# A recurrence with a capacity-dropped mixture of experts: one operand written out by ScalarE, a group's last unit fetched alone, inversion steps in four slots, late weights behind the second gather

## The chip, the cores and the metric

The kernel runs on one core of a Trainium2 chip. The metric is the device time of one execution in microseconds; lower is better. The median of three runs of the kernel before is 619.46 us (617.57 to 620.58).

## The reference, cut to what matters

The first part is a recurrence over 768 tokens for 4 batches and 8 heads with a state of 40 x 40. The second part takes its output as 3072 rows of 320, sends each row to one of 8 experts, keeps the 80 rows with the largest gate per expert, and leaves the other rows zero.

```python
for t in range(S):                                  # S = 768
    y[:, :, t] = einsum('bhd,bhde->bhe', r_t, state)
    Sa = einsum('bhde,bhe->bhd', state, a_t)
    state = state * w_t[:, :, None, :] - einsum('bhd,bhe->bhde', Sa, b_t)
    state = state + einsum('bhd,bhe->bhde', v_t, k_t)
x = y.transpose(0, 2, 1, 3).reshape(3072, 320)
logits = x @ w_gate;  expert_idx = argmax(logits, axis=1)
gate_w = softmax(logits)[arange(N), expert_idx]
for e in range(8):
    tok_idx = rows of expert e, the 80 of largest gate_w
    out[tok_idx] = gate_w[tok_idx] * (maximum(x[tok_idx] @ w1[e], 0) @ w2[e])
```

## The kernel before, in words

**Units and groups.** The recurrence is cut into chunks of 64 tokens. A unit is one chunk of two batches with all eight heads; there are 24 units, n = 0 to 23. Within a chunk the recurrence becomes a triangular system, whose matrix is called N (tile `nt`). Its diagonal blocks of 32 x 32 are inverted by elimination on VectorE, for four units at once (NG = 4): such a set of units is a group, with index k = n // 4. The elimination of a group has 30 steps, each two VectorE instructions (`step`, L381 and L384) on the tiles `lt` (the blocks) and `tt` (the inverse being built).

**The way of the blocks.** `system_kept` copies a unit's N from PSUM into `nt` on ScalarE (L352) and writes it to a DRAM tensor `blocks` with two DMAs on SP's queue (L355). When the last unit of a group has been written, `fetch` reads the blocks of all four units back as `lt`, one unit's heads on eight partitions of each block row, with four DMAs on SP (L365). `begin` makes `tt` from `lt` on GpSimd (L370). After the last step `end` writes `tt` to DRAM (`solved`, L387) and reads it back turned as `dt` (L392), both on SP. TensorE multiplies with `dt` in `diagonal` (L453).

**The order.** Each engine works through its instructions in the order in which the function `do` lays them down; SP's DMAs and those that ScalarE issues belong to that order too. The loop runs over n. In iteration n, unit n is solved, unit n - 1 is read out and its state updated, and unit m = n + 7 (AHEAD) is prepared, with the decays of m + 1. SP's loads in one iteration are, in order: `raw_w`, `blocks`, (`lt`), `raw_a`, four `raw_s`, (`solved`, `dt`), two `x_rows`, `raw_r`, `side` and, in eight iterations, a zero fill of `out`. A load of a buffer waits for the instruction that read the buffer last.

VectorE's order in an iteration is two scans (`forward`, `backward`), `decayed_a` (`ahT`), a few steps, `inverted` (`scaled`), more steps, and `summed` with `state` (L522) and `xT` (L526). The PSUM tile `yp` that `xT` reads is free for the next unit's first matmuls (L416) only after it. How many steps run is decided by `pause(steps, budget)`: it takes steps from the list until their prices exceed the budget.

```python
            if not coming:
                pause(steps, 9 if n % NG == 1 else 5.5 if n % NG == 2 else 100)
                pause(rounds_, LISTS.get(n, 0))
            elif n % NG == 0:
                do(begin, m // NG)
            else:
                pause(steps, 6.7 if n % NG < NG - 1 else 100)
```

**The start.** Before the loop, units 0 to 7 are prepared by `prepare` and `joined`, and the first group is inverted while the other engines wait for it.

**After the loop.** The gates of all rows are merged into lists of the best 80 per expert, while the weights of experts 0 to 2 are read. A chain of small instructions turns the lists into row numbers (`idx_g`). Matmuls that nobody reads (`keep_at_work`, L146, on the tile `late`) keep TensorE busy. GpSimd then gathers the rows of each expert with an indirect DMA (`gather`, L932), and TensorE does the two matrix products of each expert (`first_half` L955 and L962, `second_half` L972). A DMA of `idx_g` into a DRAM tensor `held` stands in SP's queue ahead of the weights of experts 3 to 7, so these are requested only once the row numbers exist.

Of the kernel before, what the change touches and what calls it, by code (L numbers as in the profile page):

```python
# [18 lines left out]
def kernel(  # L19
# [46 lines left out]
    assert G * ZT == 512 and NG * 32 == 128 and E == 8 and 1 <= cap <= 128  # L66
# [66 lines left out]
    ones_b = const.tile([128, 128], BF16, name="ones_b")  # L133
    behind_b = const.tile([128, 128], BF16, name="behind_b")
    seg_t = const.tile([128, E, 2 * NM], F32, name="seg")
    seg = seg_t.rearrange("p e m -> p (e m)")
    iot = const.tile([128, 1, cap], F32, name="iot")


# [7 lines left out]

    nc.gpsimd.tensor_copy(ones_b, ones)
    nc.gpsimd.tensor_tensor(out=behind_b, in0=strict, in1=ones, op=Alu.subtract)
    nc.gpsimd.memset(seg_t, 1.0)  # L150
    nc.gpsimd.memset(seg_t[:, :, 0:1], 0.0)
    iot_i = const.tile([128, cap], I32, name="iot_i")
    nc.gpsimd.iota(iot_i, pattern=[[1, cap]], base=1, channel_multiplier=0)
    nc.gpsimd.tensor_copy(iot[:, 0, :], iot_i)


    with ExitStack() as p1:
# [190 lines left out]
        def system_kept(n):  # L348
            o = of[n]
            p = o.pop("np")  # L350
            o["nt"] = nt = kept.tile([128, Z, 2 * G, T], F32, name="nt", tag="nt", bufs=AHEAD + 1)
            nc.scalar.copy(nt.rearrange("p z (q g) t -> p q z (g t)", q=2), p.rearrange("p q z g t -> p q z (g t)"))  # L352

            for i, m in enumerate(halves):
                nc.sync.dma_start(blocks[n // NG, m, n % NG], nt[m, 1 - i])  # L355
            for z, m in enumerate(halves):
                masked(nt[m, z])


        def fetch(k):  # L360
            inverse[k]["lt"] = lt = sb.tile([128, C * C], F32, name="lt", tag="lt")
            for i in range(Z):
                for j in range(NS):
                    m = block(i, j)
                    nc.sync.dma_start(lt[m].rearrange("p (s t) -> p s t", s=C),  # L365
                                      blocks[k, m, :, :, j * C : (j + 1) * C].rearrange("s u h t -> (u h) s t"))
# [183 lines left out]
        def logits_summed(n):  # L550
            i = share_of[n]
            nc.vector.tensor_reduce(logit[i][:, n - shares[i][0], :], of[n]["xb"][:, :, 2 * D :].rearrange("p g e -> p e g"),  # L552
                                    axis=AX, op=Alu.add)
            of[n].clear()
# [137 lines left out]
        def joined(n):  # L692
            do(operand, n)
            do(system, n)
            do(system_kept, n)

        def prepare(n, before=None, next_=True):
# [10 lines left out]
            if before is not None:  # L708
                do(system, before)
                do(system_kept, before)  # L710
            if next_:
# [11 lines left out]
        do(fetch, 0)  # L723
# [18 lines left out]
        for n in range(NU + 2):  # L742
# [24 lines left out]
            if coming:  # L767
                do(system_kept, m)
                if m % NG == NG - 1:
                    do(fetch, m // NG)  # L770
# [4 lines left out]
            if next_:  # L775
                do(turned_a, m + 1)
                do(decayed_a, m + 1)
            pause(small, 1)
            pause(steps, 0.7)
# [16 lines left out]
            if not coming:  # L796
                pause(steps, 9 if n % NG == 1 else 5.5 if n % NG == 2 else 100)
                pause(rounds_, LISTS.get(n, 0))
            elif n % NG == 0:
                do(begin, m // NG)  # L800
            else:
                pause(steps, 6.7 if n % NG < NG - 1 else 100)
# [19 lines left out]
            if coming and m % NG == NG - 1:  # L822
                invert(m // NG)
# [10 lines left out]
    pieces = const.tile([128, NM, NP, E], BF16, name="pieces")  # L834
    rest = const.tile([128, NM, E], F32, name="rest")
    for x, last, first_piece in ((ids, 1, 0), (gates, 4, 2)):
        for i in range(first_piece, last):
            nc.gpsimd.tensor_copy(pieces[:, :, i, :], x)
            nc.gpsimd.tensor_tensor(out=rest if i + 1 < last else pieces[:, :, last, :], in0=x, in1=pieces[:, :, i, :], op=Alu.subtract)
            x = rest  # L840

# [21 lines left out]
    with ExitStack() as p2:  # L863
# [46 lines left out]
        keep_at_work(ps_l, "still", 40, late)  # L910
# [71 lines left out]
    held = nc.dram_tensor("held", (cap, E), I32, kind="Internal")  # L982
    nc.sync.dma_start(held[:, :], idx_g)
# [37 lines left out]
```

## Time and profile before

| What | Before |
|---|---|
| Median of three runs | 619.46 us (617.57 to 620.58) |
| Profiled execution: own time, span | 620.17 us, 618.5 us |
| Mean granted TensorE clock | 0.871 |
| Busy: TensorE, VectorE, ScalarE, GpSimd | 480.6, 362.5, 234.7, 130.2 us |
| DMA: packets, of these under 512 B | 236033, 217236 |
| Inversion steps: 360 VectorE instructions, all groups | 136.4 us |

The span runs from the first to the last instruction of the program. A line of the timeline gives the start, the duration, the engine, the line of the kernel, the operation, the tiles written and read, the count of merged instructions, and in brackets the idle time of the engine before it with what ended it. A "q" after an engine's name marks its instruction queue, as in SPq, where DMAs are issued. In the list of waits the numbers are microseconds in total, times, and the longest one.

### The profile page before, as it was taken

The page shows a single profiled execution, that of the slowest core. Times are in us where ns is not written, and L with a number is a line of the kernel's source. Part 1 is how long each engine was busy: PE and PEld are TensorE (multiplying, and loading weights), DVE is VectorE, ACT ScalarE, POOL GpSimd, SP SyncE. Part 2 cuts the span into 40 slices and gives each one's busy share as a digit, 9 for nine tenths or more (in the row PEclk, how much of TensorE's full clock was granted, in tenths as well). Part 3 has the DMA queues.
Part 4 walks back from the last instruction along what each step waited for, and adds up shares of the span by engine and source line. Part 5 has one row for each costly group of instructions (what it writes and reads, how often), then busy time and mean ns, then how long its engine had stood idle before and what let it go on. Part 6 is the DMA issues. An engine that isn't in the chain of part 4 may idle for free. (4 is left out here: it accounts for less than half of the span.)

```text
span 618.5 us, 25228 instructions
## 1 busy us (share of the span) xinstructions
PE 480.6 (78%) x11281; PEld 411.2 (66%) x11281; DVE 362.5 (59%) x870; ACT 234.7 (38%) x418; POOL 130.2 (21%) x171
## 2 busy tenths in 40 slices
PE   2874039978979898978998898599888205999996
PEld 1653037867869787877887787488777204877874
DVE  8766932678547874888567853988266984001010
ACT  2462015645654655655564554154445000000000
POOL 5022003222221412422231133021112012111011
PEclk9986557989996989999998899799999556579999
DMA  4587077535777658765766345125210179995000
GB/s 75 109 165 134 11 122 124 95 64 116 137 122 145 133 128 153 144 140 96 141 113 121 73 87 103 33 70 79 49 33 14 21 258 347 330 334 158 14 14 14
DMA packets 236033, 71.46 MB, mean 116 GB/s; under 512 B 217236, under 2 KB 228756, under 8 KB 235924
## 3 DMA queue, kind: packets, MB, share of 16 engines
q1 hardware_dynamic: 223728, 66.47, 49.6%
q10 hardware_dynamic: 11428, 1.73, 1.7%
q8 instruction: 89, 1.46, 0.9%
q0 software_dynamic: 768, 1.64, 0.9%
q14 instruction: 20, 0.16, 0.1%
HBM read 51.69 MB, written 18.12 MB: 113 GB/s over the span
## 5 line engine op out<-in xcount | busy, mean ns | idle before, releaser
L272 POOL TENSOR_SCALAR_AFFINE_SELECT side<-side 64x1024 f32<-64x1024 f32 x47 | 55.3, 1176 | 113.0 <-ACT side L500 111.7
L384 DVE TENSOR_TENSOR tt<-tt,tmp 128x30 f32<-128x30 f32 (+9 forms) x180 | 71.2, 396 | 6.6
L381 DVE TENSOR_TENSOR tmp<-tt,lt 128x30 f32<-128x30 f32 (+9 forms) x180 | 65.2, 362 | 14.5 <-POOL tt L370 9.3
L272 POOL TENSOR_SCALAR_AFFINE_SELECT nt<-nt 64x512 f32<-64x512 f32 x48 | 34.4, 717 | 139.6 <-ACT nt L352 138.3
L416 PE MATMUL yp<-rT,gT 64*64 64x64 f32 x768 | 30.6, 231 | 35.9 <-DVE lg L552 28.2
L416 PEld LDWEIGHTS yp<-rT,gT 64*64 64x64 f32 x768 | 27.7, 145 | 37.8 <-issue 35.6
L319 ACT COPY qd<-qt 128x1024 f32<-128x1024 f32 x24 | 25.3, 1053 | 71.6 <-DVE qt L305 68.1
L974 DVE TENSOR_SCALAR y<-yp,weight 80x320 f32<-80x320 f32 x8 | 4.4, 548 | 79.4 <-PE yp L972 79.4
L522 DVE TENSOR_TENSOR state<-yp,pt 64x320 f32<-64x320 f32 x44 | 21.4, 487 | 50.1 <-PE yp L518 49.8
L518 PE MATMUL yp<-side,scaled 128*64 128x128 f32 (+1 forms) x768 | 47.5, 279 | 2.2 <-POOL side L272 2.2
L245 PE MATMUL tp<-ident,raw_a 128*128 128x128 f32 x96 | 19.2, 333 | 35.4 <-DMA raw_a<-in_a_dram 35.0
L518 PEld LDWEIGHTS yp<-side,scaled 128*64 128x64 f32 x768 | 41.9, 143 | 3.9 <-POOL side L272 2.4
L298 DVE TENSOR_TENSOR_SCAN pt<-decay,begins 128x520 f32<-128x520 f32 x24 | 30.3, 1263 | 20.2 <-ACT decay L292 20.0
L453 PE MATMUL pr<-yy,dt 32*32 32x40 f32 x1536 | 39.0, 203 | 3.7 <-ACT yy L446 1.8
L453 PEld LDWEIGHTS pr<-yy,dt 32*32 32x32 f32 x1536 | 32.6, 111 | 10.9 <-issue 5.7
L972 PE MATMUL yp<-w,hT 128*80 128x320 f32 x128 | 38.5, 448 | 0.0
L245 PEld LDWEIGHTS tp<-ident,raw_a 128*128 128x128 f32 x96 | 12.4, 166 | 38.5 <-issue 34.7
L966 ACT ACTIVATE hT<-hp 128x320 f32<-128x320 f32 x16 | 6.1, 434 | 83.3 <-PE hp L962 83.3
L955 PEld LDWEIGHTS hp<-xe,w 128*128 128x128 f32 x256 | 36.2, 227 | 1.5 <-issue 0.2
L955 PE MATMUL hp<-xe,w 128*128 128x80 f32 x256 | 36.4, 311 | 0.0
L266 PE MATMUL sp<-ahT,sT 64*64 64x64 f32 x1536 | 32.7, 241 | 2.3 <-ACT sT L342 2.3
L404 PE MATMUL pr<-side,nt 64*64 64x40 f32 x768 | 33.8, 235 | 0.4 <-issue 0.4
(300 smaller groups left out, 998.9 us busy)
## 6 DMA issues: line engine op xcount, KB each, us to landing
w<-in_moe_w_dram SPq DMA_DIRECT2D x8, 1280.0 KB, 14.1
w<-in_moe_w_dram SPq DMA_DIRECT2D x8, 1024.0 KB, 15.9
blocks<-nt SPq DMA_DIRECT2D x48, 128.0 KB, 2.5
raw_w<-in_w_dram SPq DMA_DIRECT2D x48, 80.0 KB, 3.2
raw_s<-in_b_dram SPq DMA_DIRECT2D x48, 80.0 KB, 2.9
raw_r<-in_r_dram SPq DMA_DIRECT2D x48, 80.0 KB, 3.1
side<-in_v_dram SPq DMA_DIRECT2D x48, 80.0 KB, 2.8
x_rows<-xb SPq DMA_DIRECT2D x48, 80.0 KB, 2.3
```

Of the source, the lines that this page charges most:

```text
L245: nc.tensor.transpose(p[:, g, :], t[:, g, :], ident)
L266: nc.tensor.matmul(p[i, q, z, g, :], lhsT=lhs[m, z, g, i], rhs=rhs[m, g, halves[z]], start=True, stop=True)
L272: nc.gpsimd.affine_select(out=o, in_=o, compare_op=Alu.is_gt, fill=0.0, base=0, pattern=[[0, o.shape[1]], [1, T]], channel_multiplier=-1)
L298: nc.vector.tensor_tensor_scan(flat(pt), flat(chunks(n)), flat(begins), 0.0, op0=Alu.mult, op1=Alu.add)
L381: nc.vector.tensor_tensor(out=tm, in0=t3[:, 0:i, i : i + 1].to_broadcast([128, i, n]), in1=l3[:, i : i + 1, i + 1 :].to_broadcast([128, i, ...
L384: nc.vector.tensor_tensor(out=t3[:, 0:i, i + 1 :], in0=t3[:, 0:i, i + 1 :], in1=tm, op=Alu.add)
L404: yield lambda h=h, z=z: nc.tensor.matmul(pr[halves[1 - z], h, :], lhsT=o["nt"][halves[z], z, of_head(n, h), :], rhs=vu[halves[z], z, h, 0:D],
L416: yield lambda z=z, g=g, m=m: nc.tensor.matmul(y[m, z, g, 0:T], lhsT=o["gT"][m, z, g, :], rhs=o["rT"][m, g, halves[z]], start=g == 0, stop ...
L453: nc.tensor.matmul(o["pr"][m, h, :], lhsT=dt_[m, (n % NG) * 2 * G + of_head(n, h), :], rhs=o["yy"][m, h, :], start=h == 0, stop=True, skip ...
L518: nc.tensor.matmul(o["y"][m, z, g, 0 : T if last else T + HB], lhsT=o["s"][:, z, 2 * g + q, :], rhs=x, start=False, stop=True, skip_group_ ...
L955: nc.tensor.matmul(hp[f // (FK // 2)][:, f % (FK // 2), :], lhsT=t1[:, i, f * 128 : (f + 1) * 128], rhs=xe[:, i, :], start=f % (FK // 2) = ...
L972: nc.tensor.matmul(yp, lhsT=hT[:, f, :], rhs=w2[:, f, :], start=f == 0, stop=f == FK - 1)
```

## The change

`system_kept` issues the two DMAs of `blocks` from ScalarE. `fetch` is called for every unit: at the third unit of a group it reads the blocks of the first three, at the fourth the blocks of that unit alone, each with four DMAs on SP; it does nothing at the first two. It stands behind `turned_a`, thus behind the load of `raw_a`. `lt` has two buffers. The steps of a group enter the list at once after `begin`, in the iteration with n % 4 == 0, and some of them run there; the budgets of the other slots are smaller, and one small budget is split around `decayed_a`. The sum of the logits moves from VectorE to GpSimd for the first 20 units, as two additions. Constants for the selection (`ones_b`, `behind_b`, `seg`, `iot`) and `pieces` are made after the loop, in a pool of their own, and not at the start. `keep_at_work` issues 52 matmuls and not 40. `held` is written from the rows of the second gather and not from `idx_g`.

```diff
-                nc.sync.dma_start(blocks[n // NG, m, n % NG], nt[m, 1 - i])
+                nc.scalar.dma_start(blocks[n // NG, m, n % NG], nt[m, 1 - i])
...
-        def fetch(k):
-            inverse[k]["lt"] = lt = sb.tile([128, C * C], F32, name="lt", tag="lt")
+        def fetch(n):
+            k, u = n // NG, n % NG
+            if u == NG - 2:
+                inverse[k]["lt"] = sb.tile([128, C * C], F32, name="lt", tag="lt", bufs=2)
+                us = slice(0, NG - 1)
+            elif u == NG - 1:
+                us = slice(u, NG)
+            else:
+                return
             for i in range(Z):
                 for j in range(NS):
                     m = block(i, j)
-                    nc.sync.dma_start(lt[m].rearrange("p (s t) -> p s t", s=C),
-                                      blocks[k, m, :, :, j * C : (j + 1) * C].rearrange("s u h t -> (u h) s t"))
+                    x = slice(m.start + 2 * G * us.start, m.start + 2 * G * us.stop)
+                    nc.sync.dma_start(inverse[k]["lt"][x].rearrange("p (s t) -> p s t", s=C),
+                                      blocks[k, m, us, :, j * C : (j + 1) * C].rearrange("s u h t -> (u h) s t"))
...
-            nc.vector.tensor_reduce(logit[i][:, n - shares[i][0], :], of[n]["xb"][:, :, 2 * D :].rearrange("p g e -> p e g"),
-                                    axis=AX, op=Alu.add)
+            lg, x = logit[i][:, n - shares[i][0], :], of[n]["xb"][:, :, 2 * D :]
+            if n < NL:
+                part = sb.tile([128, G // 2, E], F32, name="part", tag="part")
+                nc.gpsimd.tensor_tensor(out=part, in0=x[:, 0 : G // 2], in1=x[:, G // 2 :], op=Alu.add)
+                nc.gpsimd.tensor_tensor(out=lg, in0=part[:, 0], in1=part[:, 1], op=Alu.add)
+            else:
+                nc.vector.tensor_reduce(lg, x.rearrange("p g e -> p e g"), axis=AX, op=Alu.add)
...
             do(system_kept, n)
+            do(fetch, n)
...
-        do(fetch, 0)
         do(begin, 0)
...
                 do(system_kept, m)
-                if m % NG == NG - 1:
-                    do(fetch, m // NG)
...
                 do(turned_a, m + 1)
+            if coming:
+                do(fetch, m)
+            pause(steps, 0.7)
+            if next_:
                 do(decayed_a, m + 1)
             pause(small, 1)
-            pause(steps, 0.7)
+            pause(steps, 0.5)
...
-                pause(steps, 9 if n % NG == 1 else 5.5 if n % NG == 2 else 100)
+                pause(steps, 8 if n % NG == 1 else 5 if n % NG == 2 else 100)
...
                 do(begin, m // NG)
+                invert(m // NG)
+                pause(steps, 2.5)
             else:
-                pause(steps, 6.7 if n % NG < NG - 1 else 100)
+                pause(steps, 4.7 if n % NG < NG - 1 else 100)
...
-            if coming and m % NG == NG - 1:
-                invert(m // NG)
...
-        keep_at_work(ps_l, "still", 40, late)
+        keep_at_work(ps_l, "still", 52, late)
...
-    held = nc.dram_tensor("held", (cap, E), I32, kind="Internal")
-    nc.sync.dma_start(held[:, :], idx_g)
+    held = nc.dram_tensor("held", (cap, E), F32, kind="Internal")
+    nc.sync.dma_start(held[:, :], rows[1][:, 0:E])
```

The constants that move to the place behind the loop are, word for word, those made ahead of it before; only their pool is new.

## The prediction

> **What bounds the kernel now.** I read the page first, then the waits, then the timeline of one group of four units, SP's queue and the expert stage. The page has TensorE busy over most of the loop and at a lowered clock in places.
>
> ```profile
> PE   2874039978979898978998898599888205999996
> PEclk9986557989996989999998899799999556579999
> ```
>
> A slice is 15.46 us. The loop over units fills slices 6 to 31, the experts 34 to 40. Two stretches run at half clock: slices 4 to 6, and 31 to 35 with the first two experts. The list of waits names what TensorE lacks:
>
> ```profile
> PE tp L245 <- DMA raw_a<-in_a_dram: 35.0, 7, 27.5
> PE yp L416 <- DVE lg L552: 28.2, 12, 7.0
> PE xp L942 <- DMA rows<-x_rows,idx_g: 3.4, 2, 2.9
> ```
>
> The 27.5 lies ahead of the loop: the first inversion runs on VectorE while `raw_a` waits in SP's queue behind `solved` and `dt`. The 28.2 is the loop's main loss. L416 needs the PSUM that `xT` (just ahead of `lg`) frees, and VectorE does inversion steps first. A unit without any stall takes 14.0 us (199.50 to 213.52). Write t for the time from a unit's start, and slot n for the four units of a group. In slot 0 VectorE is idle; in slot 1 it is late:
>
> ```profile
> 245.94 0.99 DVE L522 TENSOR_TENSOR state<-yp,pt 64x320 f32<-64x320 f32 x2 [5.73 <-PE yp L518]
> 266.44 0.24 PE L416 MATMUL yp<-rT,gT 64*64 64x64 f32 x1 [3.00 <-DVE lg L552]
> ```
>
> So 5.6 us of steps fit after `scaled`, without harm, in any slot. SP's queue across slots 3 and 0 (unit 8 starts at 231.6) shows why slot 0 has no steps yet:
>
> ```profile
> 227.66 0.51 SPq L387 DMA_DIRECT2D solved<-tt  x1
> 231.03 2.22 SPq L392 DMA_DIRECT2D dt<-solved  x4
> ...
> 238.96 2.15 SPq L212 DMA_DIRECT2D raw_w<-in_w_dram  x2
> 241.21 1.22 SPq L355 DMA_DIRECT2D blocks<-nt  x2
> 243.72 2.94 SPq L365 DMA_DIRECT2D lt<-blocks  x4
> ```
>
> ```profile
> 249.83 1.76 POOL L370 TENSOR_SCALAR_AFFINE_SELECT tt<-lt 128x1024 f32<-128x1024 f32 x1 [9.56 <-DMA lt<-blocks]
> ```
>
> SP stands 3.4 us on the landing of `solved`, then has four `dt` and nine more DMAs ahead of the fetch: `tt` is ready at t = 20.0.
>
> Last, the experts: the 40 dummy matmuls end 2.87 us before the first gathered rows, and the first half of an expert then takes twice its later time.
>
> ```profile
> 516.91 6.45 PE L146 MATMUL still_p<-late 128*128 128x256 bf16 x40
> 526.23 0.33 PE L942 MATMUL xp<-ident,rows 80*128 80x80 f32 x2 [2.87 <-DMA rows<-x_rows,idx_g]
> 528.08 7.12 PE L955 MATMUL hp<-xe,w 128*128 128x80 f32 x32
> ...
> 562.74 3.69 PE L955 MATMUL hp<-xe,w 128*128 128x80 f32 x32
> ```
>
> **What the Trainium skill says.** "TensorE: Matmul & The Clock Gate", section "Part 1: The HAM clock gate": the array's clock falls to half after an idle window of about 3.4 us and returns after a busy one. The trace agrees: windows of the timeline show 0.50 from 528 to 546, after that 2.87 us gap, and 1.00 from 556. "DMA: Bandwidth & Descriptors", section "Issuing engines are not separate DMA queues": issuing from another engine saves only the sequencer's time. That is the gain here, since SP issues without a pause from 231 to 285. "SBUF — State Buffer", section "SBUF: two separate sides", says that VectorE and GpSimd can lock each other out of a shared port; the trace has steps of 0.41 us that take 1.22 beside GpSimd's `side` mask, so I allow a few tenths per slot.
>
> **The change, part by part.**
>
> *Steps in four slots.* By the code's own price of a step the slots had 0, 13, 10 and 7; they get 6, 9, 9 and 6. A long step pair lasts 0.82 us, 0.88 with its gaps. Slot 1 after `scaled` falls from 11 steps (9.2 us measured, against 5.6 of room) to 6 (5.2 us); slot 2 from 9 to 7, and two steps move ahead of `scaled`. The large waits at L416 in units 1 to 15 were 3.93, 2.23, 2.23, 3.00, 2.07, 2.81 and 2.10 = 18.4 us; I leave 0.5 of each: -14.9. In the tail the 6.95 at 396.85 falls to the 1.0 that every tail unit shows: -5.9. One step fewer of 0.2 us per unit (`lg` to GpSimd, idle then) lies inside this.
>
> *Clock.* The windows that hold these gaps had mean clocks of 0.91, 0.70, 0.91, 0.91, 0.91 and 0.83 over 20, 23, 18, 19, 18 and 20 us: 17.0 us lost. Gone with the gaps: -17.0, to be paid again below where new gaps come.
>
> *`raw_a` in slot 0* waited 3.26, 1.08 and 1.41 behind the fetch: it is now ahead of it, -5.7.
>
> *N from ScalarE.* Two issues took 1.30 us on ScalarE at the start of the kernel. After `nt` ScalarE idles 1.27 us for `qt` (250.56), which covers them; without that cover they would cost up to 1.3 us in each of 17 units. SP saves 1.3 us per unit. One thing is added: in the compiled kernel before, the DMAs of SP and ScalarE take eight completion counters in turn, each DMA waiting for the one eight places ahead. In slots 1 to 3 that one landed long ago. In slot 0 it is an `x_rows` or `raw_r` behind the `dt`, landing at t = 5.2 to 6.7, and ScalarE stands till then with `qd`, `yy` and so TensorE's diagonal products behind it: about 5 us of TensorE stall, in the shadow of the next item.
>
> *The fetch and slot 0, the added wait.* SP in slot 3 now: `raw_w` to 3.0, `raw_a` 4.6, three units' blocks 5.3 to 8.0, `raw_s` 8 to 11, `solved` 11.1, `dt` 14.4 to 16.6, that is t = 2.4 of slot 0. Then, at the durations above, `x_rows`, `raw_r`, `side`, `zero` to 7.5, `raw_w` 9.5, `raw_a` 11, the last unit's four DMAs 12.7, landed (2.6 to 3.5) at 15.5, `tt` 16.9. So `lt` is 3 us earlier than now, but the six steps stand in VectorE's order ahead of `state` and `xT`, which fall due at 12.6. Steps 3.6 to 4, then 1.7 for `state` and `xT`: 22.5 against 14.1, a hold of 8.4 us. With the shortest value everywhere (no delay by the three-unit fetch, 1.3 us per DMA pair, landing 2.6) it is 6; with the longest 9.5. Units 4, 8 and 12: +25.5. Unit 16: 7.6, and unit 17 with 14 steps and 1.7 of its own against 11.7: 2.5, together +10. Unit 0 has no `state` yet: +1. Each of the four long holds idles TensorE long enough for a lowered clock; part is hidden, as TensorE waits for VectorE again later: 2 us each, +8 (0 to 6.8 each; the gap at 181.81 cost 6.9).
>
> *Start.* Six GpSimd instructions (1.66 us) leave the first microseconds, where VectorE's setup is slowed by GpSimd's fills until 9.1: -1 (0 to -1.7). The first group's fetch shrinks to one unit, but the three-unit fetch now stands ahead of `raw_w` and `raw_s`, some 4 us, and the steps begin at the later of `tt` and VectorE's earlier work: -0.5 (-2.5 to +2). The constants made later on GpSimd end near 502, under VectorE's last list rounds (to 507.6), and are needed at 509.94: 0; without that cover they would cost their 1.7.
>
> *Experts.* 19 dummy matmuls ran at 0.21 us, 21 at 0.116; 12 more end at 524.8. The first gather (issued 519.34) lost its landing to 526.1 to the weights of expert 3, queued from 518.25; with these behind the second gather I take 3.7 us (the shortest landing of a gather) to 5: 523 to 524.5. No gap, so the clock stays. First half at 526.3 for 528.08: -1.8. Two first halves of 8.98 at 4.68: -8.6. Second half of expert 0, half of it slow: -1.1. Sum -11.5. The late weights start 6 us later, 13.1 MB at 0.34 MB per us end near 563; expert 3, first to need them, starts near 551 with its own there at 532, expert 7 near 590: 0.
>
> Sum: -14.9 - 5.9 - 17.0 - 5.7 + 25.5 + 10 + 1 + 8 - 1.5 - 11.5 = -12.0. The profiled execution took 620.17 us (span 618.5), 0.7 above the median: 608.2 for such a run, **607.5** as a median.
>
> **The rivals.**
> *A, the hold is as short as it can be.* For: SP was slowed by contention in the trace, and loses 2.6 us of work per two units. Against: the landing of `solved` (3.4) and the DMAs behind it remain. 2.4 less in four holds and no clock loss: 607.5 - 9.6 - 8 = 590; with half of that, 598.
> *B, the clock falls again at the experts all the same.* For: it falls on idle windows whose position I don't know, and the rows may still land late. Against: no gap of a microsecond is left. Then 10 us return: 617, no change that can be told.
> *C, slower: the hold in slot 0 pulls the clock down for as long as the one at 181.81 did.* Place: units 4, 8, 12 and 16, after `tt`. Price: 6.9 in place of 2, with 9.5 in place of 8.4 as hold: 4 x 6 = +24, 631. It decides from 3 us more per hold on, which eats the 12. For: 0.70 in unit 5. Against: the five other drops after such gaps lasted a fourth to half as long.
> That the steps don't reach slot 0 can't be: they stand in the order by hand.
>
> **How the numbers follow.** Less than 0.5% (3.1 us) a measurement can't tell. Forecast 0.55 (faster); A 0.17 (faster); B 0.13 (0.10 same, 0.02 faster, 0.01 slower); C 0.15 (0.10 slower, 0.03 same, 0.02 faster). So faster 0.76, same 0.13, slower 0.11. The range leaves out the outer half of A and of C: 594 to 621.
>
> **What would show it.** Right: `blocks` on ACT's queue with ScalarE's `qd` unmoved in slots 1 to 3; waits at L416's place of 0.5 us there, and 6 to 9 us ahead of slots 1; `tt` at t near 17; GpSimd or VectorE idle on `lt`; clock 1.00 from 526 of the old time on, and 32 `hp` matmuls in 3.7 us for all experts. Wrong: no wait on `tt` in slot 0 (then A), half clock in the first two experts (B), slices of half clock after each slot 0 (C), or a loop more than 8 us off its old length.

## The result, and the profile after

The changed kernel takes 639.04 us (median of four runs, 634.89 to 646.83) where the kernel before takes 620.02 (617.57 to 620.69): a ratio of 1.029 [1.022, 1.036]. It is slower by 19 us; 607.5 had been forecast, and the range ended at 621. The profiled execution took 634.89 us (span 633.2), 4 below the median. Runs of one kernel lie up to 25 us apart here, so ranges are given; ratios compare the runs within 1.5% of each kernel's fastest (for two kernels these are too few for an interval), and the traces of five kernels below (N on SP, the steps as before, N by GpSimd, the fetch behind `raw_a`, two steps fewer) are of runs outside that.

The lines of the changed kernel have lower numbers: L410 is L416 of the kernel before, L447 is L453, L386 (`dt`) is L392, L364 (`tt`) is L370, L520 (`xT`) is L526.

The page of the changed kernel, TensorE's busy share and its granted clock in 40 slices of 15.83 us:

```profile
PE   3865218799799996899888998587888721899997
PEclk9875557999969996799958999799998855799999
```

New dips of the clock stand in the loop at slices 12, 16 to 17 and 21 (6, 6 and 7, and 5 tenths, counting slices from 1), and the half clock of the first two experts is gone: the rows arrive in slice 35, and all slices from 36 on have 9. The waits, as total, times and longest one:

```profile
DVE tmp L375 <- POOL tt L364: 40.4, 5, 13.3
...
PE tp L230 <- DMA raw_a<-in_a_dram: 25.4, 3, 23.7
...
PE yp L410 <- DVE xT L520: 21.0, 11, 7.3
```

`raw_a` stands in the way only ahead of the loop now. TensorE's idle time ahead of L410 fell from 35.9 us (28.2 behind `lg` and 7.0 behind `xT`) to 27.6 in all, 21.0 of it behind `xT`. A new wait is VectorE's: the first step of a group waits for `tt`. Stage by stage, from the two traces:

| Stage | Before, us | After, us | Difference | Forecast |
|---|---|---|---|---|
| To the first `pr` matmul of unit 0 | 95.5 | 102.5 | +7.0 | -1.5 |
| Units 0-3, 4-7, 8-11, 12-15 | 65.2, 70.8, 65.9, 67.4 | 61.3, 72.9, 73.5, 72.2 | +10.5 | -1.7 |
| Units 16-19 | 56.8 | 63.7 | +6.8 | +2.7 |
| Unit 20 to the first gathered rows | 104.6 | 105.0 | +0.5 | 0 |
| Experts, to the end | 92.2 | 82.1 | -10.1 | -11.5 |
| Sum (spans 618.5 and 633.2) | | | +14.7 | -12.0 |

The forecast column is the prediction's sum, sorted by stage. Within a group the four slots went apart. Over units 0 to 15, those of slots 2 and 3 take 120.0 us for 139.0, those of slot 1 70.7 for 67.3, and those of slot 0 89.2 for 63.0. Units 4, 8 and 12 take 24.4, 26.3 and 24.9 us, against 15.5, 16.5 and 15.8. SP's queue of the changed kernel at unit 8, which starts at 236.69:

```profile
233.54 0.57 SPq L381 DMA_DIRECT2D solved<-tt  x1
238.70 5.79 SPq L386 DMA_DIRECT2D dt<-solved  x4
...
253.03 1.72 SPq L359 DMA_DIRECT2D lt<-blocks  x4
```

Four `dt` that took 2.22 us to issue take 5.79. The trace records which completion counter (a semaphore) each DMA raises and waits for. SP and ScalarE share eight of them, 100, 102 and 104 to 109. The second and third `dt` of this unit take 105 and 106, which the two writes of N in the same slot 0 raised last. SP reaches these `dt` ahead of the time at which ScalarE issues N, behind its `nt`. So SP stands until ScalarE has issued N and N has landed: N was issued at 240.67, the second `dt` at 242.95. It is the same in unit 4, and in unit 12 with the third and fourth. In unit 8 the first `dt` is late besides, 5.2 us after `solved` for 3.4 before. The timeline of the same unit, ScalarE, TensorE, GpSimd and VectorE one after the other:

```profile
240.67 1.10 ACTq L340 DMA_DIRECT2D blocks<-nt  x2
...
243.24 0.25 PE L447 MATMUL pr<-yy,dt 32*32 32x40 f32 x2 [1.39 <-ACT yy L440]
246.66 1.27 PE L447 MATMUL pr<-yy,dt 32*32 32x40 f32 x30 [3.16 <-DMA dt<-solved]
...
259.07 1.26 POOL L364 TENSOR_SCALAR_AFFINE_SELECT tt<-lt 128x1024 f32<-128x1024 f32 x1 [12.57 <-DMA raw_s<-in_b_dram]
...
260.37 0.19 DVE L375 TENSOR_TENSOR tmp<-tt,lt 128x30 f32<-128x30 f32 x1 [10.48 <-DMA raw_s<-in_k_dram]
...
264.97 0.69 DVE L520 TENSOR_TENSOR xT<-yp,pt 128x512 f32<-128x512 f32 x1
```

Three things are to be seen. ScalarE's `yy` is late (1.39) and then `dt` is (3.16). `tt` is ready at t = 23.6, not 16.9. And `xT`, behind the steps, comes at t = 28.3, where `state` and `xT` fell due at 12.6. The names in the last brackets are of a DMA that happened to end near; GpSimd waited for `lt`, and VectorE for `tt`. TensorE's waits for `dt` are 3.60, 3.16 and 1.97 us in units 4, 8 and 12, and those for `yy` 1.39 and 1.55 in units 8 and 12. Half clock comes with them. In unit 8 it begins at 243.51, as the wait for `dt` begins, so there it follows the late `yy` (the columns are the stretch, its length, busy time and instructions of TensorE, weight load, VectorE, ScalarE and GpSimd, granted clock, DMA share and GB/s):

```profile
171.83:185.48 13.65, 13.10 (x196) 12.14 (x198) 0.92 (x3) 4.38 (x9) 1.57 (x3) 0.50 0.73 131
...
243.51:260.58 17.07, 13.92 (x203) 12.94 (x203) 1.07 (x3) 5.15 (x11) 3.73 (x5) 0.50 0.78 129
...
318.60:332.26 13.66, 13.13 (x195) 12.17 (x197) 0.88 (x2) 4.55 (x10) 2.60 (x3) 0.50 0.70 101
```

If half of these stretches is lost, which is an estimate, they cost 6.8, 8.5 and 6.8 us. The experts do as forecast in this trace; a gap of 0.33 us is left ahead of the rows, and the first half of expert 0 takes 3.80 us for 7.12:

```profile
542.60 8.12 PE L139 MATMUL still_p<-late 128*128 128x256 bf16 x52
551.05 0.33 PE L957 MATMUL xp<-ident,rows 80*128 80x80 f32 x2 [0.33 <-DMA rows<-x_rows,idx_g]
...
552.23 3.80 PE L970 MATMUL hp<-xe,w 128*128 128x80 f32 x32
```

### The profile page after: what moved, and what is told of

Its sections match the earlier page's. It is cut to its first block, busy times and chain, and to the rows that moved or that the text cites. A ratio compares the mean times of both kernels' runs of the same rounds, so it can differ in the third digit from the quotient of the medians.

```text
span 633.2 us, 25273 instructions
## 1 busy us (share of the span) xinstructions
PE 488.2 (77%) x11293; PEld 418.2 (66%) x11293; DVE 360.1 (57%) x850; ACT 234.9 (37%) x418; POOL 147.3 (23%) x211
## 5 line engine op out<-in xcount | busy, mean ns | idle before, releaser
L375 DVE TENSOR_TENSOR tmp<-tt,lt 128x30 f32<-128x30 f32 (+9 forms) x180 | 68.5, 381 | 55.5 <-POOL tt L364 40.4
L257 POOL TENSOR_SCALAR_AFFINE_SELECT nt<-nt 64x512 f32<-64x512 f32 x48 | 41.4, 862 | 141.5 <-ACT nt L337 140.3
L447 PE MATMUL pr<-yy,dt 32*32 32x40 f32 x1536 | 41.3, 209 | 19.5 <-ACT yy L440 10.2
L512 PE MATMUL yp<-side,scaled 128*64 128x128 f32 (+1 forms) x768 | 51.7, 295 | 2.2 <-POOL side L257 2.2
L447 PEld LDWEIGHTS pr<-yy,dt 32*32 32x32 f32 x1536 | 34.8, 116 | 27.2 <-ACT yy L440 12.5
L304 ACT COPY qd<-qt 128x1024 f32<-128x1024 f32 x24 | 25.2, 1052 | 72.6 <-DVE qt L290 44.2
L410 PE MATMUL yp<-rT,gT 64*64 64x64 f32 x768 | 30.5, 231 | 27.6 <-DVE xT L520 21.0
L512 PEld LDWEIGHTS yp<-side,scaled 128*64 128x64 f32 x768 | 46.1, 153 | 4.0 <-POOL side L257 2.3
L410 PEld LDWEIGHTS yp<-rT,gT 64*64 64x64 f32 x768 | 27.5, 144 | 28.6 <-issue 25.0
L283 DVE TENSOR_TENSOR_SCAN pt<-decay,begins 128x520 f32<-128x520 f32 x24 | 29.8, 1241 | 23.7 <-ACT decay L277 22.1
L516 DVE TENSOR_TENSOR state<-yp,pt 64x320 f32<-64x320 f32 x44 | 21.4, 486 | 37.1 <-PE yp L512 36.8
L318 DVE TENSOR_TENSOR scaled<-raw_s,pp 128x320 f32<-128x320 f32 x48 | 21.2, 482 | 32.2 <-PE pp L316 30.2
L251 PE MATMUL sp<-ahT,sT 64*64 64x64 f32 x1536 | 34.3, 248 | 4.0 <-ACT sT L327 4.0
L251 PEld LDWEIGHTS sp<-ahT,sT 64*64 64x64 f32 x1536 | 30.3, 159 | 6.7 <-ACT sT L327 4.9
L316 PE MATMUL pp<-ident,qd 64*128 64x64 f32 x384 | 24.3, 273 | 12.0 <-ACT decay L277 7.7
```

Of the source, the lines that this page charges most:

```text
L251: nc.tensor.matmul(p[i, q, z, g, :], lhsT=lhs[m, z, g, i], rhs=rhs[m, g, halves[z]], start=True, stop=True)
L257: nc.gpsimd.affine_select(out=o, in_=o, compare_op=Alu.is_gt, fill=0.0, base=0, pattern=[[0, o.shape[1]], [1, T]], channel_multiplier=-1)
L283: nc.vector.tensor_tensor_scan(flat(pt), flat(chunks(n)), flat(begins), 0.0, op0=Alu.mult, op1=Alu.add)
L304: nc.scalar.copy(qd.rearrange("p g z i t -> p (g z) i t"), of[n].pop("qt")[:, :, :, 1:].rearrange("p g z t -> p (g z) t").unsqueeze(2) .to ...
L316: nc.tensor.transpose(p[:, z, g, :], qd[m, g, z, :, :].rearrange("p i t -> p (i t)"), ident[m, m])
L375: nc.vector.tensor_tensor(out=tm, in0=t3[:, 0:i, i : i + 1].to_broadcast([128, i, n]), in1=l3[:, i : i + 1, i + 1 :].to_broadcast([128, i, ...
```

## The experiments

Two theories stood against each other at first. **Theory one, late `dt`**: the completion counters that SP and ScalarE share hold `dt`, TensorE stops in the diagonal products and its clock falls. **Theory two, steps**: the steps ahead of `state` and `xT` hold slot 0 until `tt` is there. Besides, the start and the experts have runs of their own. Every time is compared with runs of the kernel before from the same session (medians of 620.97 to 623.02).

**The experts' part alone**, on the kernel before.

```diff
-        keep_at_work(ps_l, "still", 40, late)
+        keep_at_work(ps_l, "still", 52, late)
-    held = nc.dram_tensor("held", (cap, E), I32, kind="Internal")
-    nc.sync.dma_start(held[:, :], idx_g)
+    held = nc.dram_tensor("held", (cap, E), F32, kind="Internal")
+    nc.sync.dma_start(held[:, :], rows[1][:, 0:E])
```

> The kernel before with the expert part of the change alone: the small store that holds the late weights back reads rows[1] and not idx_g, and there are 52 dummy matmuls for 40. If the parts of the change add up, the experts' gain of about 10 us that the two traces show (92.3 to 82.15 from the first tokens to the end) comes whole: 620 - 10 = 610, the clock 1.0 from the first rows on, 32 hp matmuls in 3.7 us for expert 0. The rival: the gain in the changed kernel hung on its state at that time (clock or DMA load left by the loop), and here it is under 5 us: 615 or more.

613.99 us (609.29 to 623.89), ratio 0.982 [0.975, 0.989]. Both ends were seen: the fastest runs have the full 10 us, and the profiled one (616.65) has less than half of it, since its clock fell all the same. Its windows:

```profile
523.95:527.37 3.42, 2.84 (x27) 2.17 (x25) 0.81 (x2) 0.00 (x0) 1.01 (x2) 1.00 0.32 68
527.37:544.44 17.07, 17.07 (x90) 15.66 (x90) 0.00 (x0) 1.53 (x4) 0.80 (x1) 0.50 1.05 340
```

A gap of 0.58 us ahead of the rows lies in the first stretch; 17.07 us at half clock follow. In the changed kernel a gap of 0.33 did not do that. So the part is sound, but the gain from the clock is not sure: of the seven traces with 52 dummy matmuls two keep it (gaps of 0.10 and 0.33 us, 82 us for the experts), and five lose it (0.58 to 2.14 us, 90 to 96 us), those of N on SP, the steps as before, N by GpSimd and both undone among them.

**N written by SP again**, else as changed.

```diff
-                nc.scalar.dma_start(blocks[n // NG, m, n % NG], nt[m, 1 - i])
+                nc.sync.dma_start(blocks[n // NG, m, n % NG], nt[m, 1 - i])
```

> The changed kernel with N written by SP again, everywhere; all else as changed. Theory one, shared completion counters: dt no longer stands on a DMA that ScalarE has yet to issue, the four dt of units 4, 8 and 12 are issued in 2.3 us for 5.8 to 7, TensorE's waits of 2.0 to 3.6 us at the diagonal products are gone, and with them most of the 14 to 17 us of half clock in each of these units; they go from 24.4, 26.3, 24.9 to some 21, and the start gains 1 to 2 us: 639 - 12 = 627. Theory two, the inversion steps that stand ahead of state and xT: nothing of that helps, since VectorE waits for tt in any case and SP has 1.3 us more ahead of it; units 4, 8 and 12 stay at 24 to 26 and the time is 637 to 643.

649.65 us (three runs near 650, one of 634.57): neither. The `dt` are issued in 2.6 us, as theory one has it, but SP now has N and three units' blocks ahead of `solved`, which leaves at t = -0.2 in unit 8 (-3.9 before) though the last step ended at -6.0. `dt` is late by another way, the clock falls again (10.24 us in each of the three units), and the steps, with `tt` ready at 21.3 to 23.1, make TensorE wait 5.4 to 6.6 us in slot 1.

**The steps as before**, else as changed.

```diff
                 do(begin, m // NG)
-                invert(m // NG)
-                pause(steps, 2.5)
...
-                pause(steps, 4.7 if n % NG < NG - 1 else 100)
+                pause(steps, 6.7 if n % NG < NG - 1 else 100)
...
+            if coming and m % NG == NG - 1:
+                invert(m // NG)
```

> The changed kernel with the inversion steps as they were placed before: none in slot 0, the old budgets, the steps of a group entered at the end of its slot 0. Split fetch, N by ScalarE and the experts' part stay. Theory two, steps ahead of state and xT: units 4, 8, 12 fall from 25 to 14 to 16 (-30), the waits of 2.1 to 3.9 us at L410 come back in slots 1 to 3 (+15 to +20), and the time is 639 - 12 = 627 or less. Theory one, shared counters: dt still comes late and TensorE still stops at the diagonal products for 2 to 3.6 us at half clock, units 4, 8, 12 stay at 19 to 22, and with the old waits back the time is 637 to 645.

640.34 us (629.57 to 645.99), ratio 1.020 [1.009, 1.031]: theory one's side. With not one step in slot 0, units 4, 8 and 12 still take 24.8, 23.3 and 26.1 us. Its SP queue, TensorE and VectorE in unit 8 (start 244.22):

```profile
250.53 2.23 SPq L386 DMA_DIRECT2D dt<-solved  x4
...
253.46 0.31 PE L447 MATMUL pr<-yy,dt 32*32 32x40 f32 x2 [4.04 <-DMA dt<-solved]
255.36 1.27 PE L447 MATMUL pr<-yy,dt 32*32 32x40 f32 x30 [1.60 <-DMA dt<-solved]
...
265.37 0.99 DVE L516 TENSOR_TENSOR state<-yp,pt 64x320 f32<-64x320 f32 x2 [6.77 <-PE yp L512]
```

Here even the first `dt` stands: `solved` left at 241.39, ScalarE's N at 248.20, `dt` at 250.53. It takes the counter of ScalarE's N here. TensorE loses 5.64 us to it, and VectorE is idle before `state`. The steps had been in TensorE's shadow.

**The start as before**, else as changed: the first group fetched whole, N of the first seven units by SP.

> The changed kernel with the start as before: group 0 fetched whole after unit 3, and N of the first seven units written by SP; the loop as changed. If the start's 7.0 us (first pr matmul at 102.5 for 95.5) come from ScalarE's two issues per unit and from the three-unit fetch that stands ahead of raw_w, the loop starts at 95 to 97 and the time is 632 to 634. The rival, that the start shifts but the loop gives it back (it waits for VectorE's backlog at its start anyway), gives 637 to 640.

In its profile (626.89 us) the loop starts at 94.5, 8.0 earlier, and that execution is 8.0 us shorter than the changed kernel's profiled one. The four runs (median 641.18, 626.89 to 651.95, ratio 1.031 [1.022, 1.041]) don't show the gain. In three traces ScalarE writes N at the start, and their loops start at 101.6 to 102.9; in the eleven others at 94.5 to 99.9. So ScalarE's part in the later start is shown. What a late start costs in the total is not resolved, and differences under some 4.5 us tell nothing here: six kernels with the start of the kernel before lie between 95.4 and 99.9.

**N by ScalarE alone**, on the kernel before (the edit of the change, one word).

> The kernel before with one edit: ScalarE writes N (both DMAs per unit), at the start and in the loop. In this compiled kernel the dt of units 4, 8 and 12 wait for completion counters of SP's own earlier DMAs, not of ScalarE's. If ScalarE's queue by itself is harmless in the loop (the prediction's reading: qd is covered), the loop's units keep their lengths to 1 us, the dt are issued in 2.2 us, and only the start can lose: 618 to 625. The rival: 1.2 us of issue on ScalarE in each of 17 units ahead of qd are on the path, 632 or more.

630.78 us (626.26 to 633.62), ratio 1.013 [1.006, 1.020]: dearer than the prediction's reading, cheaper than the rival. The start alone is 6.1 us later (101.6). In the loop units 8 and 12 go from 16.5 and 15.8 to 21.5 and 21.3; most others keep their lengths to 2 us, but unit 5 goes from 23.3 to 16.6, unit 16 from 12.0 to 16.4 and unit 18 from 20.2 to 15.8. ScalarE and TensorE in unit 8:

```profile
238.06 1.37 ACTq L355 DMA_DIRECT2D blocks<-nt  x2
239.47 1.05 ACT L319 COPY qd<-qt 128x1024 f32<-128x1024 f32 x1 [1.44 <-issue]
240.42 0.42 ACT L446 COPY yy<-pr 128x320 f32<-128x320 f32 x1
...
240.90 0.76 PE L453 MATMUL pr<-yy,dt 32*32 32x40 f32 x32 [1.65 <-ACT yy L446]
```

In units 8 and 12 ScalarE waits for a gate's logits before `nt`, so the idle 1.27 us that were to hide the issue aren't there. `yy` is late, TensorE waits 1.65 us, and 10.24 us at half clock follow. `dt` is in time here (t = -1.0 to 1.2): in this kernel the counters of the `dt` were raised last by SP's own loads. So ScalarE's N has two costs, the late `yy` of this run and the counters, and the first alone brings half clock.

**The split fetch alone**, on the kernel before (with the constants made late, for room).

> The kernel before with the split fetch alone (three units' blocks after slot 2, the last unit's in slot 0, behind raw_a, two lt buffers; the constants made late, which makes the room for them). Theory one in its wider form, dt comes too late: the three-unit fetch stands in SP's queue of slot 3 ahead of raw_s and solved, so dt is issued 2 to 3 us later than before; it had 3 us of slack, so TensorE waits 0 to 2 us at the diagonal products, the clock falls in some of units 4, 8, 12 and these get 2 to 8 us longer: 622 to 640, with a start some 4 us later. The prediction's reading, that the fetch costs nothing and raw_a comes earlier, gives 612 to 618.

626.90 us (622.4 to 629.17), ratio 1.011 [1.004, 1.017], inside what theory one's wider form had: the start is 2.6 us later (less than can be told), and `dt` begins at t = 1.2, -3.4 and 2.4 in units 4, 8 and 12. Where it is late, in units 4 and 12, TensorE waits 1.94 and 2.24 us for it, so the slack of 3 us that the expectation gave it was too much: its issue ends 2.3 and 4.4 us later than before, which leaves 0.4 and 2.2. Units 0 to 15 in sum are level all the same in this trace, 268.8 us for 269.3.

**The steps alone**, on the kernel before: the budgets and places of the change.

> The kernel before with the step placement alone: six steps in slot 0 ahead of state and xT, fewer in slots 1 to 3. Theory two, the hold of slot 0: tt comes at t = 18 to 20 as before, steps, state and xT follow, so units 4, 8 and 12 go from 15.9 to 23 to 25 though dt is not late; slots 1 to 3 lose their waits at L410's place; 620 - 38 + 45 = 625 to 635. Theory one alone: with dt in time TensorE doesn't stop at the diagonal products, VectorE's lateness is hidden or costs under 4 us per group, and the gain of slots 1 to 3 stays: 600 to 612.

639.65 us (636.12 to 648.1), ratio 1.028 [1.019, 1.037]: theory two's side, and more than it had. `dt` is in time (2.32 us from 231.16), units 4, 8 and 12 are short (14.7, 17.8, 15.7), and the loss stands at the head of the next unit. GpSimd, VectorE and TensorE at units 8 and 9 (starts 231.72 and 249.50):

```profile
251.27 1.27 POOL L370 TENSOR_SCALAR_AFFINE_SELECT tt<-lt 128x1024 f32<-128x1024 f32 x1 [10.85 <-DMA lt<-blocks]
...
252.57 0.19 DVE L381 TENSOR_TENSOR tmp<-tt,lt 128x30 f32<-128x30 f32 x1 [11.99 <-POOL tt L370]
...
258.01 0.69 DVE L526 TENSOR_TENSOR xT<-yp,pt 128x512 f32<-128x512 f32 x1
...
258.85 0.34 PE L416 MATMUL yp<-rT,gT 64*64 64x64 f32 x1 [9.09 <-DVE lg L552]
```

VectorE idles 11.99 us for `tt`, and TensorE then waits 9.09 (11.38, 8.07 and 9.75 in the other groups).

**N by GpSimd**, else as changed.

```diff
-                nc.scalar.dma_start(blocks[n // NG, m, n % NG], nt[m, 1 - i])
+                nc.gpsimd.dma_start(blocks[n // NG, m, n % NG], nt[m, 1 - i])
```

> The changed kernel with N written by GpSimd in place of ScalarE: SP has no more work than in the changed kernel, ScalarE has less, and in the compiled kernel no dt of units 4, 8, 12 waits for a counter of another engine's DMA. Theory one, shared counters: the dt are issued in 2.3 us at t near 0 to 2, TensorE's waits of 2.0 to 3.6 at the diagonal products fall under 1, the long stretches of half clock go from units 4, 8 and 12, which fall from 25.2 to 20 to 22 (the hold of the steps stays): 624 to 630. Theory two, steps ahead of state and xT: they stay at 24 to 26 and the time is 636 to 642.

632.66 us (622.54 to 634.88), between the two. The mechanism is theory one's: `dt` is issued at once and in time. SP, GpSimd and TensorE at units 8 and 9 (starts 232.51 and 253.88):

```profile
232.28 2.24 SPq L386 DMA_DIRECT2D dt<-solved  x4
...
249.68 1.26 POOL L364 TENSOR_SCALAR_AFFINE_SELECT tt<-lt 128x1024 f32<-128x1024 f32 x1 [8.06 <-DMA lt<-blocks]
...
256.41 0.24 PE L410 MATMUL yp<-rT,gT 64*64 64x64 f32 x1 [2.27 <-DVE xT L520]
```

GpSimd's DMAs use other counters (111 to 118), so no `dt` waits for N; no diagonal product waits for `dt`, and `tt` is ready at t = 18.1, 18.4 and 16.9, near the prediction's 16.9. This edit takes away both costs of ScalarE's N, the counters and the late `yy`, so it doesn't part them. Unit 8 still takes 21.4 us: 10.24 us at half clock follow though no wait ahead of them is over 1.10 us. What is left of slot 0's loss has moved to slot 1, as in the run before (8.73 and 6.79 in units 5 and 13). The gain is larger than the total shows: unit 20 starts 16.7 us earlier than in the changed kernel, while the experts, at half clock, take 14.3 us more.

**Both undone**: steps as before and N by GpSimd.

> The changed kernel with both suspects undone at once: the steps placed as before (none in slot 0) and N written by GpSimd, so that no dt waits for another engine's DMA. Split fetch and the experts' part stay. If the late dt and the steps behind tt each suffice to hold slot 0, and so each hides the other when it is undone alone, units 4, 8, 12 fall to 16 to 18, the 11 us of steps stay out of the path, and the time is 610 to 620, below the kernel before or level with it. If a third cost of the change holds slot 0, they stay above 20 and the time is over 626.

618.19 us (614.97 to 623.77), ratio 0.993 [0.987, 1.000], as expected. Units 4, 8 and 12 take 16.2, 18.8 and 16.7 us. Slots 0 and 1 of the three groups together, from one trace each, say it best:

| Kernel | Units 4+5, 8+9, 12+13, us | Sum | Start of unit 20 |
|---|---|---|---|
| Before | 38.8, 31.6, 31.3 | 101.7 | 421.7 |
| Changed | 41.3, 43.4, 43.2 | 127.9 | 446.0 |
| Changed, steps as before | 44.2, 39.2, 41.0 | 124.5 | 448.8 |
| Changed, N by GpSimd (`dt` in time) | 40.5, 38.3, 39.3 | 118.1 | 429.3 |
| Changed, both | 31.4, 37.9, 34.8 | 104.0 | 418.8 |
| Before, steps of the change | 42.7, 43.0, 40.2 | 125.9 | 440.2 |
| Before, N by ScalarE | 33.3, 38.3, 36.7 | 108.4 | 433.2 |
| Before, split fetch | 31.5, 30.9, 34.9 | 97.3 | 422.8 |

One undone gives 3.4, the other 9.8, both 23.9: more than their sum. The steps' cost is hidden nearly whole behind the late `dt` and `yy`, that of N on ScalarE in part behind the steps. What is lost here besides the steps needs N on ScalarE and the split fetch together: N by ScalarE alone adds 6.7 us to the kernel before and the split fetch alone nothing, but with both, and the steps as before, it is 22.8. The sum of the logits on GpSimd and the constants made late stand in the kernel with both undone, which is level with the kernel before; neither has a run alone.

**Even budgets**: the kernel before with the sound parts (the experts' part with 62 dummy matmuls, `lg` on GpSimd) and smaller budgets in slots 1 and 2, and in unit 17 of the tail (6.5 for 9). Of the edit:

```diff
-                pause(steps, 6.7 if n % NG < NG - 1 else 100)
+                pause(steps, 5.5 if n % NG < NG - 1 else 100)
```

> The kernel before with the parts that the runs show to be sound: the store that holds the late weights reads rows[1], 62 dummy matmuls, lg summed by GpSimd, and the steps spread evenly over slots 1 to 3 by price (11, 8, 11 for 13, 10, 7; in the tail 12, 8, 10 for 15, 9, 6). VectorE's shortage per group stays about 6 us, but no single wait of TensorE at L416's place is over 2.5 us, so fewer windows of the clock fall to half: each group 2 to 4 us shorter, the tail 3, the experts 10 (with the longer dummy run their clock stays at 1.0): 620 - 22 = 598, 592 to 606. The rival: the waits only move from slot to slot and the clock falls as often; then the experts' gain is all: 608 to 612.

609.47 us (606.61 to 616.33), ratio 0.978 [0.973, 0.983]. The experts keep their clock, and no wait for `xT` between slots 1, 2 and 3 is over 1.2 us. But slot 3 now ends its last step at t = -0.5 to -1.2 of slot 0, TensorE waits for `dt` until 6.9 to 7.7 in units 4, 8 and 12 (2.03, 0.94 and 0.58 us), and unit 4 has 13.65 us at half clock. The trace is that of the fastest run (606.61): units 0 to 15 gain 8.2 us and the experts 9.4, but unit 20 loses 3.9 to a wait of 3.41 for `xT`, since the last group now ends in unit 19 at t = 9.5 for 4.7. So the rival's figure came, by another way than it said.

**The fetch behind `raw_a`**, on top of it.

> The same kernel with the undivided fetch of a group moved behind raw_a in SP's queue of slot 0. raw_a no longer waits behind it: the 3.26, 1.08 and 1.41 us that TensorE waited for raw_a in units 5, 9 and 13 go. tt comes 1.3 us later, at t = 20 to 21, which is 4 to 5 us into slot 1, where VectorE's first steps stand: no loss. So 4 to 6 us less than with even budgets alone. The rival: tt's delay is on VectorE's path in slot 1, the steps stand ahead of decayed_a and scaled, and the time is equal or up to 4 us more.

606.55 us (604.2 to 614.37), ratio 0.974 [0.969, 0.979]: the best version, 3 us under the last with intervals that overlap, so the step itself is not shown. Its trace has no wait for `raw_a` left in units 5, 9 and 13.

**Two steps fewer in slot 3**, on top of that (in the tail 6 for 5.5 too). Of the edit:

```diff
-                pause(steps, 5.5 if n % NG < NG - 1 else 100)
+                pause(steps, 6 if n % NG < NG - 1 else 100)
```

> The kernel with the fetch behind raw_a, with two steps fewer in slot 3: 12, 9 and 9 for 11, 8 and 11 (the tail 12, 9, 9). With 11 steps in slot 3 the last step ended 0.2 to 0.7 us ahead of slot 0 for 4.0 before, solved followed at once and dt landed at t = 7.6 to 8.2, where TensorE waited 1.0 to 1.5 us for it (units 4, 8, 12), and units 4, 8, 12 and 16 took 18 to 23. If that late dt is what is left of slot 0's loss, two steps less bring solved to t near -2.3 and dt to 5.5 to 6, its wait falls under 0.5, slot 0 to 16 to 18, and the waits of slots 1 and 2 grow by 0.7 each: 598 to 603. The rival: what one end gains the other loses, 604 to 609.

615.85 us (22 runs, 607.71 to 625.51), ratio 0.989 [0.985, 0.992]: neither, and worse than the last two; it ran on another chip, where the kernel before took 622.32. `solved` left earlier (-1.8 to -2.6), but took 3.1 to 4.7 us until `dt` could be issued, so TensorE still waited 2.01, 0.61 and 0.89 us for `dt` in units 4, 8 and 12, and the waits that follow slots 1 to 3 grew to as much as 2.0. Why one step more or less does that much is open.

## Why the prediction was wrong, by its own steps

By kind, the trace misses the forecast of -12.0 by 26.7 us as follows. Over units 0 to 19 TensorE's busy time, which grows when its clock falls (32 `hp` matmuls take 7.12 us at half clock and 3.80 at full), rose by 8.8 us, where the clock's two terms came to -9.0: 17.8 us of the miss. The start's term is 8.5 of it, and the stages from unit 20 on 1.9. TensorE's idle time rose by 8.5 where 10.0 had been reckoned, so the waits were 1.5 better than forecast. The terms that failed are thus the clock's and the start's.

**Steps in slots 1 to 3: right.** The waits at L410 that came from steps there are about 0.5 us or less, and the units of slots 2 and 3 take 14.0 to 16.5. What came back, 2.4 to 2.6 us at the head of slot 1 in units 5, 9 and 13, stands behind slot 0's late `xT`.

**`raw_a` in the loop: right.** No wait for it is left there; the 1.7 us besides the 23.7 lie in the first 15 us of the kernel.

**The completion counters: the wrong engine stood.** This is the step that failed first. The prediction had ScalarE standing on SP's DMAs, "in the shadow of the next item". It is SP that stands on ScalarE's, since N takes its counter ahead of `dt` in the compiled order and comes later in time. ScalarE issued N in 1.1 us. The price is not in a shadow. `dt` had 0.8 to 1.7 us of slack: its issue ended at t = 1.4 to 1.7 before, it is there 2.2 us later (246.66 against 244.49 in the changed kernel), and the diagonal products started at 4.7 to 5.3. Its issue now ends 4.6 to 6.1 us later. In unit 8 the counters are 3.6 of this; the rest is `solved`, which leaves and lands later.

**`tt` at t = 16.9: wrong, in the main by that.** It was ready at 21.6, 23.6 and 22.2. With N by GpSimd it was ready at 18.1, 18.4 and 16.9, so the walk along SP's queue lacked one wait and up to 1.5 us besides; with both undone it was 17.7, 22.3 and 16.7. One item of the walk varies: the first `dt` came 3.0 to 5.2 us after `solved` in these three kernels, for the 3.3 that was reckoned. (Ahead of the fetch stood eleven DMAs before, not nine, and SP paused for 1.3 us at 242.4.)

**The hold of 8.4 us: right in kind.** (Three times 8.4 is 25.2; the sum has 25.5.) Alone it shows as TensorE's 8.1 to 11.4 us at the head of slot 1, with `tt` ready at 17.9 to 20.8. In the changed kernel it lies under TensorE's half clock and shows little. So it is luck that units 4, 8 and 12 grew by 8.9, 9.8 and 9.0 us, near the 8.4 and 2 that were reckoned for each: the time went another way. For unit 0 the prediction had 1 us. There six steps hold VectorE's scan for `qt`, then ScalarE's `qd` and `yy`, TensorE waits 3.67 us, and unit 1 takes 18.4 for 13.4.

**The clock, -17.0 and +8: wrong.** The 2 us per hold were sized for a wait behind `tt`. The clock fell at t = 6.8 to 8.4, with the waits for `yy` and `dt`, and by the estimate above cost 6.8, 8.5 and 6.8 in units 4, 8 and 12. From unit 0 to unit 19 the clock was at half for 64.9 us, against 44.4 before; the sum had 9 us of lost clock less, which is 18 us less at half. With N by GpSimd it was 47.8, with the steps as before 58.0, with both undone 34.1. The price of a hold was wrong by itself too: the steps alone bring 13.65 us at half clock in unit 5 and 10.24 in units 9, 13 and 17, by the same estimate 5.1 to 6.8 us each, for 2. So rival C had the price (6.9); in the changed kernel, though, the clock fell ahead of `tt` and of the hold, not after them. The drop at 181.81 from which it took the price was not one of VectorE's: it followed the wait of 3.26 us for `raw_a`.

**The start, -1.5: wrong by 8.5.** "After `nt` ScalarE idles 1.27 us, which covers them" was read in slot 1 of the loop and doesn't hold at the start, nor in units 8 and 12. The kernel with N by ScalarE alone starts its loop 6.1 us later, the one with the split fetch alone 2.6, the changed one 7.0. SP and TensorE of the changed kernel at the start:

```profile
42.42 3.19 SPq L359 DMA_DIRECT2D lt<-blocks  x4
46.42 2.68 SPq L197 DMA_DIRECT2D raw_w<-in_w_dram  x2
...
51.42 1.09 PE L230 MATMUL tp<-ident,raw_w 128*128 128x128 f32 x4 [3.35 <-DMA raw_w<-in_w_dram]
92.31 1.09 PE L230 MATMUL tp<-ident,raw_a 128*128 128x128 f32 x4 [23.74 <-DMA raw_a<-in_a_dram]
```

The three-unit fetch stands ahead of `raw_w`, and TensorE waits 3.35 us for it; the wait for `raw_a` fell from 27.5 to 23.7, but ends at 92.3 for 86.4.

**The tail, +2.7 for +6.8.** Units 16 and 17 lost 2.1 and 7.5 us, 9.6 of the 10 that were reckoned, and unit 18 gained 6.9. What was missed is unit 19, +4.2: the last group's steps end 0.9 us ahead of it, so `solved` and `dt` (3.68 us of issue) stand ahead of two `raw_r`, TensorE waits 2.16 us for one, and 3.41 us at half clock follow.

**The experts, forecast -11.5, measured -10.1: right, with luck.** The rows came 0.33 us after the last dummy matmul, not ahead of it, and rival B, which had 0.13, is what the clock does in five of seven traces. With 62 dummy matmuls all three traces keep it.

## What to carry to other kernels

A DMA that is moved to another engine's queue also moves in the order in which the queues share their completion counters: look up in the compiled order whose DMA each urgent one has to wait for, and keep a DMA that is issued late from standing ahead of it. Ask of every transfer that TensorE needs how much slack it has (here 0.8 to 1.7 us). Two costs that lie on each other hide each other: here undoing one showed 3.4 us, the other 9.8, and both 23.9. Give the time without the clock and the time lost to the clock separate forecasts, since here the waits were right in sum and the clock was not. A cover read in one slot or stage, such as an idle engine behind an instruction, has to be read in each of the slots where the instruction runs.

## What the runs showed of the hardware

**The completion counters.** In all the traces the DMAs of SP and ScalarE use the same eight counters (100, 102, 104 to 109), and those of GpSimd eight others (111 to 118). A DMA on SP can so stand on one that ScalarE issues later in time: here four `dt` took 5.8 to 7.3 us to issue, and 2.2 with N by GpSimd. ScalarE needs 1.10 to 2.24 us to issue the two DMAs of N in the changed kernel, and `qd`, next in its order, stood 1.44 us for that with N by ScalarE alone.

**The clock.** Every complete stretch at half clock, in all fourteen traces of this case, is a whole multiple of 3.413 us, from 3.41 to 58.03, and in each trace the stretches begin on one grid of that step: 171.83, 243.51 and 318.60 in the changed kernel are 21 and 22 steps apart. The Trainium skill, "TensorE: Matmul & The Clock Gate", section "Part 1: The HAM clock gate", has a free-running window of 3413 ns, which agrees; the prediction allowed for its unknown place only at the experts.

The traces differ from the page's idle and busy windows in two points. A whole idle window isn't needed: the 2.87 us ahead of the experts in the kernel before, in which the prediction saw the page confirmed, waits of 1.65 (N by ScalarE alone) and 2.23 (unit 7 before) and even 0.58 ahead of the experts were followed by half clock. Nor does the length of the wait decide: in the kernel before, 2.10 us in unit 15 brought the clock down, and 3.00 in unit 10 did not; ahead of the experts, 0.86 and 1.01 (the two kernels with other budgets) did not. Cut along the grid, in whole windows from the start of the first unit to that of the last, the fourteen traces show a little more. Each of the 101 drops followed a window in which TensorE was busy for at most 0.71 of it (0.36 and 1.58 of 3.41 us ahead of those in units 4 and 8 of the changed kernel). Each window under 0.41 was followed by a drop, but 126 windows between 0.41 and 0.71 were not. These bounds hold for the loop alone: the window ahead of the experts' drop with their part alone was busy for 0.83 (2.84 of 3.42 us).

And the return took one window after some drops and four or five after others: behind the late `dt` and `yy`, where TensorE is shown busy for 13.1 of 13.65 us, and behind `raw_a` in unit 5 before. Each return followed a window with TensorE busy for at least 0.78 of it, but 69 windows in which it was busy throughout were followed by another at half clock. What decides both is left open.
